# Attention by query chunk over all heads, with the side work of a finished chunk list-scheduled under the next chunk's attention

## The chip, the cores and the metric

The kernel runs on one core of one Trainium2 chip. The metric is the device time of one execution in microseconds (us); a quoted time is the median of the runs named. The engines are TensorE (PE; its weight loads are PEld), VectorE (DVE), ScalarE (ACT), GpSimd (POOL) and SyncE (SP, which issues the DMAs).

## The reference, cut to what matters

Two layers, each an attention block and a feed-forward block (FFN), share their weights. The sequence has 2048 rows of width 512, 32 heads of width 16, and an FFN width of 1792, all in bf16.

```python
x = A_x
for layer in range(2):
    q, k, v = split(layernorm(x) @ wqkv)              # 32 heads of 16
    p = softmax(q @ k.T * 16 ** -0.5)                 # 32 x 2048 x 2048
    x = x + (p @ v) @ wo
    x = x + gelu_tanh(layernorm(x) @ w1 + b1) @ w2 + b2
```

The softmax needs 2 x 32 x 2048 x 2048 exponentials. The kernel works on cells of 128 keys by 512 queries of one head, three cells to one ScalarE instruction, a *unit* below: 4096 cells, 1366 units. The denominator comes from a column of ones beside V.

## The kernel before: the parts that the change and the argument touch

A helper records every operation with what it reads and writes, and inserts semaphore waits; each engine executes its list in order. The stages follow each other: projections, attention, FFN, attention, FFN. Attention goes by *quad* of heads outermost, so no chunk of rows is finished until the last quad:

```python
def attention_core(self):
    for g in range(NQUAD):                 # 8 quads of 4 heads
        for qc in range(NC4):              # 4 chunks of 512 queries
            for kt in range(NT):           # 16 tiles of 128 keys
                for a in range(4):
                    cells.append((g, qc, kt, a))
    ...
    for step in range(U + LEAD):           # a unit is 3 cells
        if self.proj_queue: ...            # every 6th step: one projection, 4 matmuls in a row
        emit_scores(step)                  # 3 matmuls of 32 rows, side by side in the array
        emit_pv(step - LEAD)
        emit_exp(step)                     # ScalarE: 128x1536 exp out of PSUM
```

```python
# Q has a padded copy of its weights (8 x 128 columns), the output projection too (8 row blocks)
T["WQp"] = sb([128, NDC, 8, 128], BF16, "wqp")
T["WOq"] = sb([128, 8, D], BF16, "woq")
...
# FFN: bias and half on ScalarE, products of GELU on DVE, tanh on ScalarE
self.AHX[i] = P.add("act", lambda e, ...: e.activation(
    out=T["XB"][:, xs, :], in_=hp, func=ACT.Identity, bias=T["HB1T"][:, fc:fc + 1], scale=0.5), ...)
...
def run(self):
    for rep in range(2):
        self.attention_core()
        ffn = self._FFN(self, ...)         # output projection, norm and FFN of chunk c+1 beside the FFN of chunk c
        ...
```

The softmax here doesn't subtract the row's maximum and nothing guards it: scores larger than these inputs give would overflow.

## Time and profile before

| | before |
|---|---|
| time, median of 3 runs | 2415.55 us (2415.5 to 2415.96) |
| ScalarE busy | 2075.6 us, 86% |
| TensorE busy | 1996.8 us, 83% |
| exp: instructions, spacing in an undisturbed stretch | 1366, 1.347 us |
| floor of the exps alone, 1366 x 1.347 us | 1840 us |

The first lines are from the profile's page of the kernel before: busy time by engine, ScalarE's busy share in 40 equal slices (tenths), the granted TensorE clock in the same slices (tenths of full speed, 9 is 90% or more), and the costliest group, with busy time, mean duration in ns, and idle time of the engine before it.

```profile
span 2415.9 us, 23401 instructions
...
PE 1996.8 (83%) x10145; PEld 463.8 (19%) x10145; DVE 523.7 (22%) x1087; ACT 2075.6 (86%) x1763; POOL 23.4 (1%) x26
...
ACT  3799999999999999933448889999999999998344
...
PEclk9855555555555555588986665555555555555899
...
L513 ACT ACTIVATE pt<-ps 128x1536 bf16<-128x1536 f32 (+1 forms) x1366 | 1841.8, 1449 | 28.4 <-PE ps L530 27.9
...
```

A group's mean duration is not its pace: an exp lasts 1449 ns and starts 1.347 us after the one before, as neighbours overlap by some 0.10 us. (The Trainium skill, "ScalarE: Activation LUTs", section "What ACT_TABLE_LOAD costs", gives 93 ns for this overlap; the trace has 1449 - 1347 = 102 ns, which is close.)

Next is the table by stage of the kernel before. Its columns are the stretch in us, its length, then busy us and number of instructions of PE, PEld, DVE, ACT and POOL, the granted clock, and the DMA share and rate.

```profile
0.00:100.00 100.00, 67.90 (x314) 30.52 (x315) 25.14 (x67) 46.04 (x78) 10.59 (x14) 0.95 0.24 79
100.00:1020.00 920.00, 777.22 (x4095) 138.83 (x4093) 94.79 (x155) 918.77 (x684) 0.00 (x0) 0.50 0.00 1
1020.00:1280.00 260.00, 206.00 (x924) 86.08 (x921) 157.00 (x373) 114.75 (x193) 8.51 (x8) 0.88 0.00 1
1280.00:1470.00 190.00, 152.31 (x794) 32.35 (x794) 28.96 (x45) 162.06 (x120) 0.00 (x0) 0.64 0.00 1
1470.00:2228.00 758.00, 641.63 (x3374) 114.27 (x3372) 79.58 (x131) 757.22 (x563) 0.00 (x0) 0.50 0.00 1
2228.00:2416.00 188.00, 151.74 (x656) 61.72 (x654) 138.23 (x317) 76.75 (x128) 4.25 (x4) 0.90 0.04 12
...
```

The second and fifth line are the attention stages. ScalarE is busy without a gap, TensorE is busy 84% of the time, and its clock is half. In the first, third and last line ScalarE is busy 41% to 46% of the time and runs no exps, or nearly none. In the fourth line projections are put among the exps. All that is not the pace of exp is 2416 - 1840 = 576 us: about 103 us of head, 254 between the layers, 188 at the end, and by subtraction 31 in the fourth stretch.

Now the timeline of TensorE in that fourth stretch: start, duration, line, shapes, count. L442 is the burst of four full matmuls of a projection, L501 the scores, L530 P·V.

```profile
1280.84 0.60 PE L530 MATMUL ps<-pt,v 128*17 128x512 bf16 x3
1281.37 1.89 PE L442 MATMUL ps<-xlnt,wqp 128*128 128x512 bf16 x4
...
1283.70 0.39 PE L530 MATMUL ps<-pt,v 128*17 128x512 bf16 x3
...
1286.98 0.61 PE L501 MATMUL ps<-qtp,ktc 32*128 32x512 bf16 x3 [0.63 <-ACT pt L513]
...
1309.98 1.89 PE L442 MATMUL ps<-xlnt,wkc 128*128 128x512 bf16 x4
1311.80 0.61 PE L501 MATMUL ps<-qtp,ktc 32*128 32x512 bf16 x3
...
1315.03 0.60 PE L530 MATMUL ps<-pt,v 128*17 128x512 bf16 x3
...
```

Two bursts behave differently. After the first, three P·V matmuls take 0.39 us instead of 0.60, until 1286.98: the clock doubled for about 3.4 us. After the second nothing changes. The Trainium skill ("TensorE: Matmul & The Clock Gate", Part 1) has the clock either half or full, judged in free-running windows of 3.4 us. The trace fits that: the changes of pace stand on a grid of 3.41 us, the first burst lies whole in one window, and the second is split by the grid's point at 1310.9 into 0.94 and 0.95 us. A count over all 57 windows of this kind between 1277 and 1471 us, from the trace's clock records, says more. Each of the 12 windows with 1.55 us or more of these full matmuls was followed by a window at full clock, and none of the 38 with 0.95 us or less was. Of the 7 between (1.14 to 1.36 us) 3 were: those in which TensorE, with scores and P·V counted in, was busy for 3.3 us or more; in the other 4 it was busy for 3.0 us or less.

### The profile page before, as it was taken

Reading aid. Unit: us, or ns where it says so; the run is one execution under the profiler, and the core shown is the slowest. Engines: PE = TensorE matmul, PEld = TensorE weight load, DVE = VectorE, ACT = ScalarE, POOL = GpSimd, SP = SyncE. Lnnn points to the kernel's source line nnn. Section 1 sums busy time; section 2 is a strip of 40 time slices with the busy share of each in tenths; the row PEclk is TensorE's granted clock in tenths of the full one; section 3 lists DMA queues with packets and bytes.
Section 4 is the critical chain, followed back from the end, with each engine's and each line's share of the span. In section 5 each row is a group of like instructions: output and inputs, shape, how many; then the busy total and the mean of one; then the engine's idle time right before and its main releaser. Section 6 shows DMA issues by size and latency. Waiting matters only on the chain.

```text
span 2415.9 us, 23401 instructions
## 1 busy us (share of the span) xinstructions
PE 1996.8 (83%) x10145; PEld 463.8 (19%) x10145; DVE 523.7 (22%) x1087; ACT 2075.6 (86%) x1763; POOL 23.4 (1%) x26
## 2 busy tenths in 40 slices
PE   5888888888888888877888878888888888888787
PEld 2311111111111111133332111111111111111333
DVE  3011111111111111167551111111111111111687
ACT  3799999999999999933448889999999999998344
POOL 1000000000000000000000000000000000000000
PEclk9855555555555555588986665555555555555899
DMA  4000000000000000000000000000000000000000
GB/s 131 1 1 1 1 1 1 1 1 1 1 1 1 1 1 1 1 1 1 0 1 1 1 1 1 1 1 1 1 1 1 1 1 1 1 1 1 1 18 18
DMA packets 9254, 11.46 MB, mean 5 GB/s; under 512 B 702, under 2 KB 8639, under 8 KB 9151
## 3 DMA queue, kind: packets, MB, share of 16 engines
q1 hardware_dynamic: 9150, 9.97, 1.3%
q8 instruction: 79, 1.29, 0.2%
q14 instruction: 25, 0.20, 0.0%
HBM read 7.87 MB, written 2.10 MB: 4 GB/s over the span
## 4 chain that ended last, share of the span: by engine, by line
ACT 76%; PE 16%; DVE 7%; issue 1%; DMA 0%; SPq 0%; POOL 0%; DVEq 0%
ACT pt L513 74%; PE ps L442 4%; PE ps L682 3%; PE ps L627 2%; PE ps L599 2%; ACT xlnt L403 1%; DVE xb L671 1%; PE ps L448 1%; PE ps L396 1%; DVE x L653 1%; PE ps L501 1%; DVE x L649 1%; PE ps L530 1%; DVE stats L323 1%; DVE x L694 1%
## 5 line engine op out<-in xcount | busy, mean ns | idle before, releaser
L513 ACT ACTIVATE pt<-ps 128x1536 bf16<-128x1536 f32 (+1 forms) x1366 | 1841.8, 1449 | 28.4 <-PE ps L530 27.9
L501 PE MATMUL ps<-qtp,ktc 32*128 32x512 bf16 x4096 | 821.3, 595 | 297.4 <-ACT pt L513 296.4
L530 PE MATMUL ps<-pt,v 128*17 128x512 bf16 x4096 | 814.1, 590 | 1.0 <-ACT pt L513 1.0
L582 DVE COPY xs<-ps 128x512 f32<-128x512 f32 x64 | 44.2, 691 | 1554.2 <-PE ps L530 1554.2
L501 PEld LDWEIGHTS ps<-qtp,ktc 32*128 32x128 bf16 x4096 | 143.0, 99 | 978.5 <-ACT pt L513 967.6
L530 PEld LDWEIGHTS ps<-pt,v 128*17 128x17 bf16 x4096 | 133.9, 91 | 588.2 <-issue 576.8
L638 ACT ACTIVATE xb<-ps,hb1t 128x512 bf16<-128x512 f32 x112 | 77.0, 687 | 150.5 <-PE ps L627 150.5
L682 PE MATMUL ps<-w,xb 128*128 128x512 bf16 x448 | 123.7, 402 | 15.4 <-DVE x L694 10.3
L627 PE MATMUL ps<-xlnt,w 128*128 128x512 bf16 x448 | 122.9, 399 | 1.4 <-ACT xlnt L403 1.4
L403 ACT COPY xlnt<-ps 128x512 bf16<-128x512 bf16 x64 | 37.4, 585 | 100.2 <-PE ps L396 100.2
L396 PE MATMUL ps<-ident,xln 128*128 128x128 bf16 x256 | 30.1, 253 | 70.3 <-ACT xlnt L403 40.2
L671 DVE SCALAR_TENSOR_TENSOR xb<-x,xb 128x512 bf16<-128x512 bf16 x112 | 76.4, 684 | 0.5 <-ACT x L661 0.5
L442 PE MATMUL ps<-xlnt,wqp 128*128 128x512 bf16 x256 | 74.1, 437 | 0.8 <-DVE xs L582 0.8
L599 PE MATMUL ps<-woq,otn 128*128 128x512 bf16 x256 | 69.0, 418 | 5.7 <-DVE x L603 5.7
L661 ACT ACTIVATE x<-x 128x512 bf16<-128x512 bf16 x112 | 69.5, 620 | 1.4 <-DVE x L653 1.3
L649 DVE TENSOR_TENSOR x<-xb 128x512 bf16<-128x512 bf16 x112 | 47.1, 421 | 78.2 <-ACT xb L638 74.8
L682 PEld LDWEIGHTS ps<-w,xb 128*128 128x128 bf16 x448 | 42.8, 102 | 79.5 <-DVE xb L671 18.7
L627 PEld LDWEIGHTS ps<-xlnt,w 128*128 128x128 bf16 x448 | 45.1, 102 | 62.1 <-issue 15.0
L442 PE MATMUL ps<-xlnt,wkc 128*128 128x512 bf16 x128 | 43.0, 491 | 7.2 <-ACT xlnt L403 3.5
L653 DVE TENSOR_TENSOR x<-x,xb 128x512 bf16<-128x512 bf16 x112 | 47.6, 425 | 3.8
L583 DVE STREAM_TRANSPOSE xt<-xs 128x512 f32<-128x512 f32 x64 | 45.5, 711 | 2.2
L592 DVE STREAM_TRANSPOSE otn<-xs 128x512 bf16<-128x512 bf16 x64 | 45.5, 711 | 2.2
(41 smaller groups left out, 468.1 us busy)
## 6 DMA issues: line engine op xcount, KB each, us to landing
w<-in_B_w_dram SPq DMA_DIRECT2D x2, 1792.0 KB, 12.6
x<-in_A_x_dram SPq DMA_DIRECT2D x1, 2048.0 KB, 8.4
out_dram<-x SPq DMA_DIRECT2D x4, 512.0 KB, 3.8
xb<-in_A_wqkv_dram SPq DMA_DIRECT2D x1, 512.0 KB, 9.4
wkc<-in_A_wqkv_dram SPq DMA_DIRECT2D x1, 512.0 KB, 8.7
wvc<-in_A_wqkv_dram SPq DMA_DIRECT2D x1, 512.0 KB, 8.8
woq<-in_A_wo_dram SPq DMA_DIRECT2D x32, 16.0 KB, 2.8
b1c<-in_B_b_dram SPq DMA_DIRECT2D x1, 3.5 KB
```

Of the source, the lines that this page charges most:

```text
L442: e.matmul(pb, lhsT=lhsT, rhs=XLNT[:, dc, cols], start=(dc == 0), stop=(dc == NDC - 1)))
L501: fns.append(lambda e, o=o, lhsT=lhsT, rhs=rhs, a=a: e.matmul(o, lhsT=lhsT, rhs=rhs, start=True, stop=True, tile_position=(32 * a, 0)))
L513: AEXP[s] = P.add("act", lambda e, src=src, r=r, n=n: e.activation(out=PT[:, r, 0:n, :], in_=src, func=ACT.Exp, scale=0.25), reads=[self.P ...
L530: fn = (lambda e, o=o, lhsT=lhsT, rhs=rhs, kt=kt, a=a: e.matmul(o, lhsT=lhsT, rhs=rhs, start=(kt == 0), stop=(kt == NT - 1), tile_position ...
L599: fns = [(lambda e, g=g: e.matmul(YP, lhsT=T["OTN"][:, g, t * 128:(t + 1) * 128], rhs=T["WOq"][:, g, :], start=(g == 0), stop=(g == NQUAD ...
L627: fns = [(lambda e, hp=hp, dc=dc, fc=fc, tc=tc: e.matmul(hp, lhsT=T["W1"][:, dc, fc * 128:(fc + 1) * 128], rhs=T["XLNT"][:, dc, tc * 512:( ...
L638: self.AHX[i] = P.add("act", lambda e, hp=hp, xs=xs, fc=fc: e.activation(out=T["XB"][:, xs, :], in_=hp, func=ACT.Identity, bias=T["HB1T"][ ...
L649: P.add("dve", lambda e, XB=XB, X2=X2: e.tensor_tensor(out=X2, in0=XB, in1=XB, op=ALU.mult), reads=[xb], writes=[x2])
L653: self.DZ[i] = P.add("dve", lambda e, XB=XB, X2=X2: e.tensor_tensor(out=X2, in0=X2, in1=XB, op=ALU.mult), reads=[x2, xb], writes=[x2])
L661: self.AT[i] = P.add("act", lambda e, X2=X2: e.activation(out=X2, in_=X2, func=ACT.Tanh), reads=["X2.%d" % x2s], writes=["X2.%d" % x2s])
L671: self.DG[i] = P.add("dve", lambda e, XB=XB, X2=X2: e.scalar_tensor_tensor(out=XB, in0=X2, scalar=1.0, in1=XB, op0=ALU.add, op1=ALU.mult), ...
L682: fns = [(lambda e, t4=t4, G=G, fc=fc: e.matmul(Y[t4], lhsT=G[:, t4 * 128:(t4 + 1) * 128], rhs=T["W2"][:, fc, :], start=(fc == 0), stop=Fa ...
```

## The change

The intent is to keep ScalarE on exps from the start to the end. Queries are taken chunk by chunk over all heads, so that after one chunk's attention its output projection, norm, FFN, second norm and the projections of the next layer can be done while ScalarE works on the next chunk's exps. K and V are kept per layer for that. Each piece of work is a coroutine that yields operations with a guessed cost; a list scheduler simulates the engines with those guesses and fixes the order on each engine when the program is built. Side matmuls are yielded one at a time, to fall into the gaps between scores and P·V.

```diff
-        for g in range(NQUAD): for qc ...: for kt ...: for a in range(4): cells.append(...)
+    def passes(self):
+        for l in range(NL):
+            cut = 4 if l == 0 else NT - 4
+            out += [(l, 0, g, range(cut), False, False) for g in range(8)]      # first chunk in two parts
+            out += [(l, 0, g, range(cut, NT), True, True) for g in range(8)]
+            for qc in range(1, self.NQ):
+                out += [(l, qc, g, range(NT), False, True) for g in range(8)]
...
+MM = 0.30                                   # guessed cost of one side matmul, us
+class _Sched: ...                           # picks, per engine, the ready operation of best priority
...
+        s.pool("misc", [7, 3, 4, 5])        # PSUM banks of the side work; 3, 4, 5 go to the scores later
+        s.pool("pv", [6])
+        s.pool("s", [0])                    # one score slot of 3 banks, a second after the first layer's K and V
...
+        for h in range(4):                  # projections, output projection, FFN: one matmul per operation
+            yield _Op("pe", MM, fns[h:h + 1], reads=reads, writes=["B.%d" % b])
+        yield _Op("dve", DV, ...)           # every copy out of PSUM is on DVE
...
+        yield _Op("pool", 2.2, lambda e: e.tensor_tensor(out=x2, in0=g2, in1=g2, op=ALU.mult), ...)
+        yield _Op("pool", 0.8, lambda e: e.tensor_scalar(x2, x2, 8.0 * C2, 2.0 * C1, ...), ...)
+        yield _Op("pool", 2.2, lambda e: e.tensor_tensor(out=x2, in0=x2, in1=g2, op=ALU.mult), ...)
+        yield _Op("act", 1.05, lambda e: e.activation(out=x2, in_=x2, func=ACT.Tanh), ...)
...
-        T["WQp"], T["WOq"]                  # padded weights
+        yield _Op("pool", 0.5, lambda e, ...: e.tensor_scalar(   # Q is padded by a mask, one quad at a time
+            T["QP"][:, s, :], T["Q"][:, b, 512 * qc:512 * qc + 512], T["MASK"][:, t:t + 1], None, op0=ALU.mult), ...)
```

P·V now goes in groups of four cells instead of three, and the full matmuls of Q and of the output projection are halved, from 512 to 256 for the two together over both layers.

## The prediction

> **What bounds the kernel now.** The page gives a span of 2415.9 us, ScalarE (ACT) 86% busy, TensorE (PE) 83%. The chain of waits is 74% exp (1366 activations; in the stretch 103 to 1023 us they follow each other every 1.347 us and nothing else matters: the stage table shows ACT 100%). The rest of the span, some 500 us, is stages where exp is idle or starved: 0-103 us (norm and projections), 1023-1277 us and 2228-2416 us (output projection, norms, FFN; ACT 45-60%), and 1277-1466 us, where projections are put between exps as bursts of four matmuls and an exp unit takes 9.6/6 = 1.60 us. So the floor is 1366 x 1.347 = 1840 us of exp.
>
> **What the change does.** Queries go chunk by chunk over all heads, so output projection, norm, FFN and the next layer's K/V/Q of a finished chunk can run under the next chunk's exps. PSUM copies, the FFN bias and half leave ACT for DVE; three GELU multiplications go to GpSimd; ACT keeps exp and 56 tanh of 1024 columns (about 1.0 us each from the 1024-column exp's 1023 ns; one table load in the trace serves both functions). Padded copies of W disappear: full-array matmuls fall from 256+128+128+256 (Q, K, V, output) to 512; with 896 of the FFN and 32 of the bias 1440. P·V goes in groups of four.
>
> **PE is the new limit.** In the attention stages the granted clock is 0.50; three score matmuls or one P·V group take 0.54 us start to start (timeline), against 0.32 where it is 1.0. A full matmul takes 0.43 or 0.216 us, plus about 0.11 us after a change of tile form. In the built order about 950 of the 1366 units carry one full matmul each: 0.54 + 0.75 x 0.54 + 0.54 = 1.5 us of PE when throttled, 0.9 at full clock, against 1.35 of ACT. The Trainium skill ("TensorE: Matmul & The Clock Gate", Part 1) has the clock either half or full, decided in windows of 3.4 us; the trace agrees: a burst with 1.4 us or more of full matmuls in one window gave 3.4 us of full clock, one split 0.8/1.0 us gave none. The new order puts about 1.0 us in a window: marginal. I expect 0.6 to 0.75 granted in mixed stretches and about 1.47 us per unit there.
>
> **Sum (estimate).** First exp at 25 us; first 50 units (176 full matmuls among them, one score slot only) 95; 950 mixed units x 1.47 = 1400; 366 plain units x 1.35 = 494; tail after the last exp 70 (output projection, norm, seven GELU pairs in series on GpSimd, about 5.5 us each by the Trainium skill, "GPSIMD Engine Reference", section 3.1: 2.6 cycles per element with two inputs; no such op is in this trace). About 2085, and 10 for waits on the single PSUM bank of the side work: **2095 us**, range **2025 to 2180**. Chances: faster 0.98, same 0.01, slower 0.01.
>
> **What would show it.** ACT busy about 1900 us, 90%; no stretch of ACT under 60% but the first 50 us and the last 70; exp spacing 1.35 us with clock 0.50 in units 50-170, about 1.4-1.55 in mixed stretches with ACT waiting for PE; PE busy over 90% there; DVE about 25%; GpSimd some 300 us, only critical in the tail.
>
> **What would make it wrong.** Mixed stretches at full clock: ACT bound, about 2010. Never above 0.5: 2130 to 2180. The static order is made with guessed costs; if DVE or GpSimd are later than guessed, PE, in order, stalls with scores behind a waiting matmul.

## The result, and the profile after

| | before | after |
|---|---|---|
| time, median of 4 runs each | 2415.76 us | 2084.75 us (2081.38 to 2087.55) |
| ratio | | 0.8627, interval 0.8614 to 0.8639 |
| ScalarE busy | 2075.6 us, 86% | 1916.8 us, 92% |
| TensorE busy | 1996.8 us | 1720.5 us |
| GpSimd busy | 23.4 us | 445.3 us |
| mean granted clock | 0.602 | 0.681 |

A ratio here and below is the mean time of one kernel's runs over that of the other's runs of the same rounds, so it is not quite the ratio of the medians that are quoted.

The same lines of the page for the changed kernel, with two GpSimd groups added: the masking of Q (L717) and the second product of GELU (L617).

```profile
span 2083.7 us, 22456 instructions
...
PE 1720.5 (83%) x9889; PEld 393.9 (19%) x9889; DVE 514.0 (25%) x875; ACT 1916.8 (92%) x1423; POOL 445.3 (21%) x274
...
ACT  4799999999999999999999959999999999999951
...
PEclk9955556876577855875578755778557775778556
...
L759 ACT ACTIVATE pt<-ps 128x1536 bf16<-128x1536 f32 x1366 | 1867.6, 1582 | 91.0 <-PE ps L741 67.9
...
L717 POOL TENSOR_SCALAR qp<-q,mask 128x512 bf16<-128x512 bf16 x80 | 125.3, 1566 | 1146.1 <-PE ps L741 1138.4
...
L617 POOL TENSOR_TENSOR x<-x,g 128x1024 bf16<-128x1024 bf16 x56 | 120.9, 2159 | 4.2
...
```

ScalarE is at 90% or more in nearly all slices; the two valleys of before are gone and one slice with a 5 is left. The clock line is no longer 5 throughout the attention. The table by stage of the changed kernel, with the columns of before:

```profile
0.00:20.00 20.00, 8.29 (x45) 4.02 (x45) 12.43 (x32) 2.73 (x2) 7.38 (x13) 1.00 0.96 321
20.00:101.00 81.00, 69.43 (x461) 23.25 (x458) 48.22 (x99) 59.50 (x41) 15.43 (x11) 1.00 0.06 19
101.00:280.00 179.00, 134.05 (x802) 24.31 (x802) 20.23 (x38) 178.53 (x134) 16.36 (x10) 0.51 0.00 1
280.00:1207.00 927.00, 817.10 (x4640) 184.77 (x4636) 233.57 (x390) 900.31 (x667) 207.93 (x124) 0.69 0.00 1
1207.00:1236.00 29.00, 22.51 (x79) 4.78 (x76) 7.67 (x12) 8.10 (x7) 1.56 (x1) 0.57 0.00 1
1236.00:2009.00 773.00, 621.95 (x3728) 136.41 (x3728) 157.01 (x256) 760.26 (x569) 155.91 (x94) 0.68 0.01 3
2009.00:2084.00 75.00, 47.18 (x152) 16.34 (x148) 34.86 (x51) 7.39 (x7) 40.74 (x22) 0.66 0.02 7
...
```

Line by line: 20 us, near the end of which the first exp starts (at 18.3 us; at 103 before); a head of 81 us in which only 41 exps run (41 x 1.34 = 55 us, so 26 lost); a plain stretch at half clock, in which the exps start every 1.340 us; the first mixed stretch; a hole of 29 us, in which ScalarE is busy for 8; the second mixed stretch; and a tail of 75 us after the last exp (188 before). What is left above the exps is 2084 - 1366 x 1.340 = 254 us. Of it 20 + 26 + 75 are named; the waits of ScalarE between 100 and 2008 us name most of the rest (who waited for whom: total us, times, longest):

```profile
ACT pt L759 <- PE ps L741: 30.5, 147, 1.0
ACT pt L759 <- PE ps L785: 20.7, 4, 7.1
ACT x L618 <- POOL x L617: 7.5, 7, 1.5
```

The second line is the hole, 21 us. The third is tanh waiting for GpSimd. The first is exp waiting for scores, 30.5 us in 147 pieces; each such piece also loses the overlap of 0.10 us with its neighbour, so it costs about 45 us. With 49 tanh between the exps at 0.95 us of pace each, 47 us, that makes 20 + 26 + 75 + 21 + 7.5 + 45 + 47 = 242 of the 254 (an estimate in its last three terms).

So 576 us above the exps became 254. Under the exps the side work now costs about 100 us, tanh included, besides the hole, where it cost 254 + 31 and most of the end.

Where does exp wait for scores? The table sorts slices of 10 us of the changed kernel's trace by the side work that dominates in them. It is worked out from the timeline and the clock of each slice; exps are counted by their starts.

| dominating side work | us | granted clock | full matmuls per unit | us per exp |
|---|---|---|---|---|
| none | 510 | 0.51 | 0.03 | 1.34 |
| output projection | 160 | 0.58 | 0.94 | 1.43 |
| projections of layer 2 (with the hole) | 260 | 0.57 | 1.16 | 1.60 (without the hole 1.47) |
| first FFN matmul, with tanh on ScalarE | 480 | 0.74 | 1.25 | 1.53 (0.12 of it tanh) |
| second FFN matmul | 470 | 0.84 | 1.25 | 1.40 |

At about 1.0 full matmul per unit the clock stays near half, and the exps come slower than 1.34; at 1.25 it is mostly full. The count per unit is not all, though: the projections (1.16) and the second FFN matmul (1.25) differ little in it and much in the clock, 0.57 and 0.84. That their matmuls fall differently into the windows would explain it, but was not tested apart.

### The profile page after: what moved, and what is told of

Read it like the earlier page. It is cut to its first block, busy times and chain, and to the rows that moved or that the text cites. A ratio compares the mean times of both kernels' runs of the same rounds, so it can differ in the third digit from the quotient of the medians.

```text
span 2083.7 us, 22456 instructions
## 1 busy us (share of the span) xinstructions
PE 1720.5 (83%) x9889; PEld 393.9 (19%) x9889; DVE 514.0 (25%) x875; ACT 1916.8 (92%) x1423; POOL 445.3 (21%) x274
## 4 chain that ended last, share of the span: by engine, by line
ACT 58%; PE 33%; POOL 5%; DVE 4%; issue 1%; DMA 0%; POOLq 0%
ACT pt L759 56%; PE ps L741 12%; PE ps L785 8%; PE ps L600 3%; PE ps L496 3%; PE ps L581 2%; PE ps L631 2%; POOL x L617 2%; ACT x L618 2%; PE ps L493 2%; POOL x L614 1%; PE ps L472 1%; POOL x L615 1%; DVE stats L448 1%; POOL qp L717 1%
## 5 line engine op out<-in xcount | busy, mean ns | idle before, releaser
L759 ACT ACTIVATE pt<-ps 128x1536 bf16<-128x1536 f32 x1366 | 1867.6, 1582 | 91.0 <-PE ps L741 67.9
L741 PE MATMUL ps<-qp,kt 32*128 32x512 bf16 x4096 | 719.3, 520 | 304.2 <-ACT pt L759 295.4
L785 PE MATMUL ps<-pt,v 128*17 128x512 bf16 x4096 | 539.9, 517 | 8.5 <-DVE v L511 3.8
L717 POOL TENSOR_SCALAR qp<-q,mask 128x512 bf16<-128x512 bf16 x80 | 125.3, 1566 | 1146.1 <-PE ps L741 1138.4
L741 PEld LDWEIGHTS ps<-qp,kt 32*128 32x128 bf16 x4096 | 140.5, 96 | 884.2 <-ACT pt L759 687.7
L600 PE MATMUL ps<-xf,w 128*128 128x512 bf16 x448 | 182.8, 476 | 8.0 <-DVE g L606 6.8
L631 PE MATMUL ps<-w,g 128*128 128x512 bf16 x448 | 174.4, 469 | 16.2 <-DVE g L619 15.9
L614 POOL TENSOR_TENSOR x<-g 128x1024 bf16<-128x1024 bf16 x56 | 107.9, 1928 | 232.1 <-DVE g L606 230.6
L606 DVE TENSOR_SCALAR g<-ps,hb1t 128x512 bf16<-128x512 f32 x112 | 83.3, 747 | 206.2 <-PE ps L600 205.8
L617 POOL TENSOR_TENSOR x<-x,g 128x1024 bf16<-128x1024 bf16 x56 | 120.9, 2159 | 4.2
```

The source lines that it names most:

```text
L600: fns = [lambda e, dc=dc, fc=fc, pb=pb: e.matmul(pb, lhsT=T["W1"][:, dc, fc * 128:(fc + 1) * 128], rhs=T["XF"][:, dc, :], start=(dc == 0), ...
L614: yield _Op("pool", 2.2, lambda e: e.tensor_tensor(out=x2, in0=g2, in1=g2, op=ALU.mult), reads=gk, writes=xk)
L617: yield _Op("pool", 2.2, lambda e: e.tensor_tensor(out=x2, in0=x2, in1=g2, op=ALU.mult), reads=gk + xk, writes=xk)
L631: fns = [lambda e, fc=fc: e.matmul(pb, lhsT=T["G"][:, fc, q], rhs=T["W2"][:, fc, :], start=(fc == 0), stop=False) for fc in range(NFC)]
L717: yield _Op("pool", 0.5, lambda e, s=s, b=b, t=t, qc=qc: e.tensor_scalar(T["QP"][:, s, :], T["Q"][:, b, 512 * qc:512 * qc + 512], T["MASK" ...
L741: fns.append(lambda e, o=o, lhsT=lhsT, rhs=rhs, a=a: e.matmul(o, lhsT=lhsT, rhs=rhs, start=True, stop=True, tile_position=(32 * a, 0)))
```

## The experiments

All runs gave correct results, with the one exception that is named. Times are medians of 4 runs; a difference is to the 2084.75 us of the changed kernel, taken on another occasion, and every run was timed beside the kernel before, whose median stayed between 2415.8 and 2416.9 us.

**My theory** was: under the exps ScalarE is nearly the limit everywhere, and what it loses to TensorE is lost because one side matmul per unit is just too little activity to hold the full clock. **Rivals:** TensorE's amount of work is what costs (then its order hardly matters, and more work costs more); or the 331 us come mainly from relieving ScalarE of its PSUM copies, not from the overlap.

### Denser side matmuls: `e1_mm020`

```diff
-MM = 0.30
+MM = 0.20
```

> Only the guessed cost of one side matmul in the list scheduler is lowered from 0.30 to 0.20 us, so the same matmuls stand denser between the exps (units with two or more: 329 instead of 208; units with none 727 instead of 533). Theory (clock): in the changed kernel the mixed stretches lose about 49 us to ScalarE waiting for a TensorE that is throttled because one full matmul per unit is just too little activity in a window of the clock gate; denser side work trips the full clock (mean granted clock in stretches with side work up from about 0.7 to 0.85 or more), and the time falls by 15 to 40 us, to 2045-2070. Rival (work): TensorE's total work is the same and its order hardly matters, or longer bursts stall scores as in the kernel before: 2080-2130.

Measured: 2058.11 us, 26.6 less (ratio to before 0.8517). The clock in slices with projections rose from 0.57 to 0.84, with the output projection from 0.58 to 0.72. The waits of ScalarE between 100 and 1982 us:

```profile
ACT pt L759 <- PE ps L741: 27.4, 80, 1.1
ACT x L618 <- POOL x L617: 18.5, 18, 1.8
```

The time falls into the range of the clock theory, but the waits say that this run alone does not prove it: the hole's line (20.7 us) is missing altogether, which is most of the gain. Waits for scores fell only from 147 to 80 pieces, and tanh waits 11 us longer for GpSimd, whose work came closer together too. The run shows that order matters at equal work; the clock has to be shown apart.

### Sparser side matmuls: `e2_mm038`

```diff
-MM = 0.30
+MM = 0.38
```

> The same guess raised to 0.38 us, so side matmuls stand sparser in the busy stretches but run into later units. Theory (clock): fewer windows trip the full clock, mean clock of mixed stretches falls toward 0.6, each mixed unit takes about 1.5 us, and the work that no longer fits before the layer boundary widens the hole there: 2100-2140. Rival (work): within 10 us of 2085 but for the hole.

Measured: 2100.61 us, 15.9 more (0.8689), and the result was **wrong** (relative error 0.118), which was not intended. The time is therefore only an indication; the direction fits both theories, as the hole grew. The mean granted clock, 0.704, did not fall as I had expected. A cause was found in the program, though no run with it mended was made. A listing made while this program was built, of who last wrote each buffer when a reader was placed, finds that tile 0 of the normalised attention output was overwritten by the norm of chunk 3 before the output projection of the row tiles 9, 10 and 11 (of chunk 2) was placed. The same listing of the changed kernel finds no such case. The recording layer orders operations only as they were placed, and this tile has one copy and no pool that hands it out. So in this design a wrong guess of a cost can give a wrong result.

### Useless matmuls added: `e3_fill`

```diff
+            fz = [lambda e, h=h: e.matmul(pb, lhsT=T["ZERO"][:, :], rhs=..., start=False, stop=False)]
-            yield _Op("pe", MM, fns[h:h + 1], ...)
+            yield _Op("pe", MM, fz + fns[3:4] if h == 3 else fns[h:h + 1] + fz, ...)
```

> Work is ADDED: in the groups of the second layer's projections and of the output projection, each full matmul gets a companion with an all-zero stationary tile accumulating zeros into the same bank (320 useless full matmuls, results unchanged). Those stretches run at clock 0.50 in the changed kernel, with exp every 1.39 to 1.5 us. Theory (clock): two full matmuls per unit trip the full clock there (0.9 to 1.0 instead of 0.50) and the exps come every 1.35 us in them; about 20 us won there, some 5 to 10 us lost in the layer boundary and the tail where the companions only add: 2065-2085. Rival (work): 320 x 0.43 us more on an engine that is already the limit there: plus 60 to 130 us, 2145-2215.

Measured: 2070.12 us, 14.6 **less** (0.8567), with 320 full matmuls more. This is the run that separates the theories: the rival that counts work had expected at least 60 us more. The table by stage, in both kernels where projections of layer 2 run; first the changed kernel,

```profile
740.00:790.00 50.00, 50.00 (x240) 9.49 (x236) 8.94 (x15) 47.13 (x34) 1.56 (x1) 0.50 0.00 1
...
```

then this one:

```profile
730.00:780.00 50.00, 42.63 (x293) 10.55 (x297) 8.92 (x14) 50.00 (x39) 1.56 (x1) 1.00 0.00 1
...
```

In the changed kernel TensorE is busy for all 50.00 us at clock 0.50, and 34 exps touch the stretch. With twice the side matmuls it is busy 42.63 us at clock 1.00, ScalarE has no gap, and 39 exps touch it. Over all slices dominated by the output projection the clock rose from 0.58 to 0.90 and the pace of exp from 1.43 to 1.35 us. The waits of ScalarE from 100 to 1990 us:

```profile
ACT pt L764 <- PE ps L746: 21.4, 76, 0.9
ACT pt L764 <- PE ps L790: 20.4, 3, 6.9
...
```

The hole is as wide as before (20.4 us); waits for scores fell from 30.5 us in 147 pieces to 21.4 in 76. That is 9.1 us and, with 71 lost overlaps of 0.10, about 16 us: the whole gain.

### Q projections last: `e6_qlast`

```diff
-            if l == 1 or c == 0:
+            if c == 0:
                 units.append(("Q", b))
...
-        if l == 0 and c > 0:
+        if c > 0:
             units += [("Q", b) for b in range(4)]
```

The hole in the changed kernel, on the timeline of ScalarE (start, duration, idle time before it and its releaser):

```profile
1209.71 2.79 ACT L759 ACTIVATE pt<-ps 128x1536 bf16<-128x1536 f32 x2 [0.91 <-PE ps L785]
1219.47 1.45 ACT L759 ACTIVATE pt<-ps 128x1536 bf16<-128x1536 f32 x1 [6.97 <-PE ps L785]
1228.03 1.45 ACT L759 ACTIVATE pt<-ps 128x1536 bf16<-128x1536 f32 x1 [7.11 <-PE ps L785]
1235.22 5.48 ACT L759 ACTIVATE pt<-ps 128x1536 bf16<-128x1536 f32 x4 [5.74 <-PE ps L785]
```

Between these exps K, Q and V groups pass one after another through the single side bank: four matmuls, then a DVE copy of 0.69 us during which TensorE waits. V and K of the last chunk are what the first pass of layer 2 waits for.

> In the second layer the Q projections of a chunk other than the first are put after its K and V projections. In the changed kernel ScalarE idles about 21 us near 1207-1236 us, where the last chunk's K, Q and V groups pass one by one through the single side bank, four of them Q groups of about 2.7 us that nothing waits for. Theory: the hole shrinks by 8 to 11 us, total 2074-2078. Rival: the hole is set by the norm of the chunk and by PV order, not by the number of groups in it: within 3 us of 2085.

Measured: 2076.85 us, 7.9 less (0.8597). The hole's line became:

```profile
ACT pt L759 <- PE ps L785: 10.0, 3, 4.4
...
```

The theory holds: 10.7 us less of hole gave 7.9. The code already sets a lower priority for Q. It does not act here, because banks are handed out in the order of the coroutines' creation and not by priority; that part is read from the code, not measured.

### FFN bias back on ScalarE: `e4_bias_act`

```diff
-            yield _Op("dve", DV, lambda e, fc=fc, pb=pb: e.tensor_scalar(...,  op0=ALU.add, op1=ALU.mult), ...)
+            yield _Op("act", 0.60, lambda e, fc=fc, pb=pb: e.activation(
+                out=T["G"][:, fc, :], in_=pb, func=ACT.Identity, bias=T["HB1T"][:, fc:fc + 1], scale=0.5), ..., prio=2)
```

> One part of the change undone: the FFN bias and half (112 evictions of 128x512) go back from DVE to ScalarE (0.69 us each in the trace of before, about 0.59 where they follow another activation). Theory (ScalarE is within 5 per cent of being the limit everywhere under the exps, the throttled TensorE costs only the rest): plus 45 to 66 us, 2130-2151. Rival (TensorE is the limit in the mixed stretches, so ScalarE has room): plus 0 to 25 us, 2085-2110. Rival (relieving ScalarE is what gave the 331 us): plus 100 or more.

Measured: 2114.62 us, 29.9 more (0.8755): between my range and the rival's. (In this run and in those with a split tail the bias is halved once at the start.) The waits of exp between 100 and 2040 us:

```profile
ACT pt L759 <- PE ps L741: 26.8, 139, 0.6
ACT pt L759 <- PE ps L785: 12.1, 3, 5.2
...
```

Of the 112 evictions 98 lie under the exps; at 0.59 us they are 58 us. The waits give back part: the hole shrank from 20.7 to 12.1, waiting for GpSimd from 7.5 to 0.4, for scores from 30.5 to 26.8 us, together 19.4 of the 28 us by which the run stays below 58; the rest stays open. So ScalarE is the limit under the exps less strictly than I had written: about a third of the added work is seen to fall into its waits, and nearly half cost nothing.

### PSUM copies back on ScalarE: `e5_copies_act`

```diff
-            yield _Op("dve", DV, lambda e: e.tensor_copy(T["K"][l][:, i, cols], pb), ...)
+            yield _Op("act", 0.55, lambda e: e.copy(T["K"][l][:, i, cols], pb), ..., prio=2)
             # the same for Q, V and the transposed norm
```

> Another part undone: the PSUM copies of the projections and of the normalised transposes (160 of 128x512) go back from DVE to ScalarE. 64 of them fall in the first 100 us, where ScalarE is idle half of the time, so they should cost little; the 96 others about 0.49 us each. Theory (ScalarE limit): plus 35 to 55 us, 2120-2140. Rival (TensorE limit): plus 0 to 20. Together with the bias run it says how much of the gain is relief of ScalarE (expected about 100 of 331) and how much the overlap itself.

Measured: 2111.45 us, 26.7 more (0.8745), again below my range. The exp's waits between 100 and 2000 us:

```profile
ACT pt L759 <- PE ps L741: 18.8, 85, 0.9
...
ACT pt L759 <- PE ps L785: 1.7, 3, 0.7
...
```

The 96 copies under the exps are 96 x 0.49 = 47 us; the hole is 19 us smaller and waiting for scores 11.7 smaller, and the copies themselves wait 9.2 us for TensorE (1.6 more for GpSimd): 47 - 19 - 11.7 + 9.2 + 1.6 = 27. (With the 62 fewer lost overlaps, counted as for `e3_fill`, it is 21; the profiled runs differ by 22.8, the medians by 26.7.) The two runs together: relieving ScalarE is worth about 57 of the 331 us, if the two parts add, which no run with both tests. The rival that takes it for the main gain falls.

### The kernel before with the bias on DVE alone: `b1_before_bias_dve`

```diff
-            self.AHX[i] = P.add("act", lambda e, ...: e.activation(..., func=ACT.Identity, bias=..., scale=0.5),
+            self.AHX[i] = P.add("dve", lambda e, ...: e.tensor_scalar(T["XB"][:, xs, :], hp, 0.5, T["HB1T"][:, fc:fc + 1],
+                op0=ALU.mult, op1=ALU.add),
```

> The kernel before with one part of the change alone: the FFN bias and half (112) go from ScalarE to DVE, nothing is overlapped. Theory (the gain comes from running side work under the exps; relieving ScalarE is worth something only there): no gain, within 1 per cent of 2416 or slower, as the FFN stages have ScalarE idle half of the time and DVE at 55 to 66 per cent: 2410-2450. Rival (relief of ScalarE is worth its busy time anywhere): minus 60 to 77, 2340-2355.

Measured: 2461.9 us (ratio to before 1.0189), 46 us slower, somewhat more than I had allowed. (By the 2% mark of the record this counts as unclear, but the interval, 1.0174 to 1.0204, leaves no room for a gain.) The same move that is worth 30 us under the exps costs 46 us in the serial FFN, where ScalarE had idle time and DVE is on the chain of waits: 13% of it here, 7% before.

### The tail over three engines: `e7_tail_split`

In the chain of waits that ended last, the largest part of the tail of the changed kernel, some 36 of 75 us, is the three GELU steps on GpSimd, for seven pairs (start, duration, engine, line):

```profile
...
2045.37 1.90 POOL x L615
2047.35 1.89 POOL x L614
2049.24 2.08 POOL x L617
...
```

```diff
+        last = l == NL - 1 and c == self.NQ - 1     # only then: bias on ScalarE, square and scale on DVE
+        ge, k1, k2 = ("dve", 0.75, 0.45) if last else ("pool", 2.2, 0.8)
-        yield _Op("pool", 2.2, ... in0=g2, in1=g2 ...)
+        yield _Op(ge, k1, ... in0=g2, in1=g2 ...)
```

> Only for the last chunk of the last layer, after which no exp is left: FFN bias on ScalarE, the GELU square and scale on DVE, only the last product on GpSimd. Theory: the tail of 75 us after the last exp is paced by seven pairs in series on GpSimd at 5.3 us (37 us); spread over three engines a pair takes about 2.6 us at most and the time falls by 12 to 22 us, to 2063-2073. Rival: the tail is paced by TensorE at half clock (56 plus 60 matmuls of 0.43 us are 50 us): within 5 us of 2085.

Measured: 2073.97 us, 10.8 less, with wide runs (2067.92 to 2085.2; ratio 0.8589, interval 0.8558 to 0.8621). The profiled run's tail was about 62 us instead of 75. One of the four runs was no faster, and the interval just touches that of the changed kernel (0.8614 to 0.8639), so the shorter tail of the profile is what shows the direction and speaks against the rival; the size is below my lower end. The spread has a pattern: 2067.92 us came with a mean granted clock of 0.696, 2085.2 us with 0.666, and in the changed kernel and every run here but `e11_combo015` the fastest of the four is the one with the highest clock (or shares it). How one and the same program meets the free-running windows may be the reason, but that was not tested. In the new chain the largest line is DVE's last GELU step, two of them in a row (3.2 us), so the pace moved at least partly from GpSimd to DVE.

### Two score slots, one side bank in the head: `e12_head`

```diff
-        s.pool("misc", [7, 3, 4, 5])
-        s.pool("s", [0])
+        s.pool("misc", [7])
+        s.pool("s", [0, 1])
-        s.spawn(self.handback(), 3)
```

> The changed kernel with one part altered: two score slots from the start and only one PSUM bank for side groups, instead of one slot and four banks until the first layer's K and V are there. In the changed kernel exps come every 1.97 us between 20 and 100 us. Theory (the single score slot makes exp and scores take turns): the spacing falls below 1.6 us at once, but the projections then pass through one bank at about 2 us a group and starve the exps later, so the stage ends within 15 us of where it did: 2070-2100. Rival (TensorE's own work paces the head, 69 of 80 us busy at full clock): spacing stays near 1.9.

Measured: 2134.93 us, 50.2 more (0.8838); a miss in size. Two stretches of the table by stage of this run:

```profile
50.00:100.00 50.00, 41.90 (x287) 11.89 (x287) 17.34 (x34) 46.85 (x35) 10.72 (x7) 0.76 0.00 1
100.00:150.00 50.00, 34.22 (x139) 8.50 (x135) 13.15 (x19) 14.14 (x11) 0.21 (x1) 0.74 0.00 0
...
```

In the first, 35 exps start in 50 us, every 1.36 us on average. But this does not settle what set the 1.97 us of the changed kernel, because the side work fell as well: there 4.0 full matmuls were done per exp (from 50 to 100 us), here 0.7. Nor did the spacing fall at once: between 20 and 50 us only 8 exps ran. The timeline of the changed kernel in its head says more:

```profile
63.75 0.39 PE L741 MATMUL ps<-qp,kt 32*128 32x512 bf16 x3 [0.26 <-ACT pt L759]
...
64.19 1.45 ACT L759 ACTIVATE pt<-ps 128x1536 bf16<-128x1536 f32 x1 [0.49 <-PE ps L741]
...
```

Scores wait for the exp that holds the slot, and the next exp waits 0.49 us for the scores: 1.45 + 0.49 = 1.94 us, the usual spacing there. So the turns of the single slot pace the head. TensorE is idle for only 0.26 us of such a round, however, so with two slots and as much side work its own work alone would have needed some 1.7 us (an estimate from these lines): the rival was nearly right too.

In the second only 11 exps touch 50 us: the exps had run ahead of the projections, which pass through one bank, and the longest wait was 27.9 us. Between 20 and 330 us ScalarE waited 87 us for TensorE, against 22 in the head of the changed kernel. Trading one slot for three side banks was better than this; I had put the cost of the single bank far too low.

### Candidates: `e8_combo`, `e11_combo015`, `e10_combo030`

`e8_combo` joins MM = 0.20, Q last, the split tail, and guesses for GpSimd set to what the trace measured.

```diff
-MM = 0.30
+MM = 0.20
-            yield _Op("pool", 0.5, ...)      # masking of Q
+            yield _Op("pool", 1.6, ...)
-        yield _Op("pool", 2.2, ...); _Op("pool", 0.8, ...); _Op("pool", 2.2, ...)
+        yield _Op(ge, k1, ...); _Op(ge, k2, ...); _Op("pool", 2.3, ...)     # pool: 2.1, 1.35
```

> A candidate that beats both: guessed side matmul 0.20 us, Q groups of the second layer last, the last chunk's FFN split over three engines, and the GpSimd guesses set to what the trace of the changed kernel measured (2.1, 1.35, 2.3 us for the GELU steps, 1.6 for the padding of Q). Theory (the parts are separate): 27 from the denser order and the closed hole, 10 to 12 from the tail, and a few from tanh waiting less for GpSimd: 2035-2050. If the parts overlap: 2050-2060.

Measured: 2025.73 us, 59.0 less than the changed kernel (0.8376 of before), correct: faster than both kernels and than I had expected. The waits of ScalarE between 100 and 1962 us:

```profile
ACT pt L766 <- PE ps L748: 29.1, 69, 2.1
ACT x L625 <- POOL x L624: 1.3, 4, 0.4
```

No hole is left, tanh hardly waits for GpSimd, and scores are waited for in 69 pieces instead of 147; the tail is about 60 us. That the GpSimd guesses matter shows against `e1_mm020`, where tanh waited 18.5 us.

`e11_combo015` is the same with MM = 0.15.

> The same candidate with the guess at 0.15 us: 336 units carry two side matmuls, 74 one. Clock theory: two per unit already hold the full clock, so little more is to be had, while bursts of three and more and tanh packed closer start to stall exps: within 12 us of the 0.20 candidate. If density were the whole story it would win another 15 us or more.

Measured: 2026.05 us (0.8385): no difference. Setting side matmuls closer than 0.20 brought nothing more here.

`e10_combo030` leaves MM at 0.30 and adds the zero-weight companions instead.

> The same candidate with the guess left at 0.30 us, but the zero-weight companions in the second layer's projections and the output projections: the clock raised by useless work rather than by a denser order. From the runs alone: 2085 minus 15 (companions) minus 8 (Q last) minus 11 (tail) minus a few (tanh): 2045-2055.

Measured: 2047.95 us, 36.8 less (0.8476), inside the range: the parts add up. Its hole is still 9.8 us wide. Real work set closer beats useless work by 22 us, of which the hole, closed in `e8_combo`, can explain about 10.

## Why the prediction was right

The time was right: 2095 predicted, 2084.75 measured, 0.5% off. That it came so close is partly luck: the mixed stretches came out about 59 us shorter than their term of 1400, and the plain units (about 390 at 1.34 us instead of 366 at 1.35, an estimate) and the hole together about 52 us longer than theirs.

- **The floor.** The exps kept their pace, 1.340 us in the plain stretch after 1.347 before; 1366 of them are 1830 of 2084 us. Right.
- **Head and first exp.** 25 predicted and 18 measured; then 95 us for the first 50 units and about 92 measured, with the single slot visible as the pace in the timeline (under `e12_head`).
- **Mixed units.** 1.47 us predicted; measured 1.46 without the hole (1341 us for 918 exps in the slices with side work). The size is right, in part by luck, as the make-up differs: I derived it from a TensorE that needs 1.5 us per unit at half clock and called TensorE the new limit. That is the part of the mechanism that did not hold: ScalarE stayed nearly the limit, and work added to it cost over half of its time (`e4_bias_act`: 29.9 of 58 us, `e5_copies_act`: 26.7 of 47). The number of units was high, too: 950 against 918, and the expectation of `e1_mm020` counts only 833 units with any side matmul in the built order. Measured, about 0.05 us per unit is tanh, and waiting for TensorE is another 0.05. I had named tanh, but not put it beside the waits. The clock over the two mixed stretches, 0.69 and 0.68, lay in the range of 0.6 to 0.75.
- **The clock is marginal.** Shown by `e3_fill`: more work, less time, with the clock from 0.50 to 1.00 in the same stage.
- **The tail.** 70 us predicted, 75 measured; a GELU triple on GpSimd 5.5 predicted, 1.93 + 1.25 + 2.16 = 5.34 measured. Right. Outside the tail ScalarE waited for GpSimd for only 7.5 us, though the chain of waits leads through GpSimd for 5% of the span, some 100 us, of which only about 36 are in the tail.
- **Waits on the side bank: 10 us, measured 21 in one place.** This term was mis-sized: I had spread it evenly, and it sat at the layer boundary, where nothing but that bank's groups could run (`e6_qlast`). The line that no stretch but the two ends would have ScalarE under 60% is wrong for the same reason.
- **GpSimd busy some 300 us: 445 measured.** Of the missing 145 us, 125 are the masking of Q, which I had left out: 80 x 1.566 us. It cost little: the profile puts 3.5 us of waits of TensorE and its weight loads down to it, though 8 of the 80 stand on the chain.
- **TensorE busy over 90% in the mixed stretches:** 88% and 80% measured, at a clock of 0.69 and 0.68.
- **What the gain is made of.** Relief of ScalarE is about 57 of 331 us (`e4_bias_act`, `e5_copies_act`, added). The rest, some 270 us, follows by subtraction and holds the overlap, the shorter head and the halved matmuls of Q and of the output projection; these I did not separate. The single move of one part into the kernel before makes it slower (`b1_before_bias_dve`).

## What to carry to other kernels

When one engine's floor is 1840 of 2416 us, first list the stages in which that engine idles, and put their work under its own; moving small work off it can come after: here the move of the FFN bias cost 46 us before the overlap and gained 30 us after it. A TensorE that is busy all the time by the clock on the wall can still be throttled: look at its granted clock by stage, and try setting side matmuls closer before adding or removing any. In a statically scheduled kernel read the trace back into the guessed costs, and give every single-copy buffer a pool or a token, as otherwise a guess decides whether the result is right.

## What the Trainium skill lacked or had wrong

- "TensorE: Matmul & The Clock Gate", Part 1 says that the gate follows how busy the PE has recently been, and advises against idle gaps. It lacks, for matmuls other than transposes, that those using a part of the array count for less: here TensorE was busy 50.00 of 50 us at clock 0.50, with scores of 32 rows, P·V of 17 columns and one full matmul per unit, and two full matmuls per unit gave 1.00 at 42.63 us busy. It names no share of a window that trips the gate; in the kernel before, 0.95 us or less of full matmuls in a window of projections among exps never did, and 1.55 us or more always did.
- The same page, Part 1, warns that zero operands do not trip the current limiter. It does not say how they count for the clock gate: matmuls with an all-zero stationary operand raised the clock from 0.50 to 1.00 (`e3_fill`).
- "GPSIMD Engine Reference", section 3.1, gives 2.6 cycles per element with two inputs, 2.2 us for 1024 elements: the product took 2.16 us, which agrees, and the square, which reads one tensor twice, 1.93 us. Section 4.1 calls one-input operations roughly line-rate: scale and add by constants took 1.25 us for 1024 elements, and multiplying 512 elements by a scalar per partition 1.57 us, which at the page's 1.2 GHz are 1.5 and 3.7 cycles per element. That the last takes over twice as long per element is on no page that I read; whether the scalar per partition is the reason was not tested apart.
- "ScalarE: Activation LUTs", section on table sets, has exp and tanh in one set: the trace agrees, with one table load of 1.28 us in the whole run although the two alternate.
